# Transposes of the identity in TensorE's gaps up to the first step, with new due dates up to step 16

## Chip, cores and metric

One core of a Trainium2 chip. The metric is the device time of one execution in microseconds (us), the median over several runs. Engines: PE = TensorE, DVE = VectorE, ACT = ScalarE, POOL = GpSimd, SP = SyncE, which here only issues transfers.

## What is computed

A linear attention feeds a two-layer feed-forward block. With q, k, v of 8 batches, 8 heads, 576 rows, 64 columns, in float32 (eps is 1e-9):

```python
q_s = exp(q - max(q, over d));  q_s = q_s / (sum(q_s, over d) + eps)
k_s = exp(k - max(k, over s));  k_s = k_s / (sum(k_s, over s) + eps)
kv  = einsum('bhsd,bhse->bhde', k_s, v)
x   = einsum('bhsd,bhde->bhse', q_s, kv)      # heads side by side: 4608 x 512
h   = x @ w_in                                # w_in 512 x 2048
out = (s * relu(h)**2 + b) @ w_out            # w_out 2048 x 512
```

## The kernel before

**Tiling.** The rows of x are cut into nine blocks of 512: eight hold the first 512 rows of each batch, the ninth gathers the remaining 64 rows of all batches. The hidden size of 2048 is cut into 16 chunks of 128, so there are 9 x 16 = 144 steps. Every product of the feed-forward part is made in three pieces, high x high, high x low and low x high, since weights and x are each split into a rounded high part and a remainder. A step is 12 matmuls into one bank of PSUM, `h` (line 693), an elementwise chain over ACT and DVE that gives `gh` and `gl` (lines 718 to 735), and 12 matmuls into `acc` (line 760).

**The start.** Before step 0 the attention of batch 0 has to be done, in units `u` of two heads, two units to a pair. A unit of K (`k_stream`, line 324) is turned by five transposes on PE (`kT`, line 330), its maximum is taken on DVE (`km`, line 333), exp on ACT gives `ke` (line 338), five more transposes turn it back (`kn`, lines 343 and 344), and ACT copies it out (lines 346 and 347). A unit of q (`q_stream`, line 400) has its maximum, subtraction, exp, sum and scaling on DVE and ACT (lines 409 to 423), is turned on PE (`qT`, line 427), copied by ACT (`qf`, line 430) and multiplied by `kv` (`xp`, line 437); ACT and DVE then write x in its two parts (lines 443 and 446). `kv` itself is 20 small matmuls a pair (line 295). The transposes take the 128 x 128 identity `ident` as their second operand.

**The weights.** Each of the 16 chunks comes in two transfers of 512 KB (`load_w`, lines 180 and 182) and is converted by `conv_w` in seven operations on ACT and DVE (lines 196 to 219), chunk 0 in two halves. All of block 0's steps wait for these conversions, so that DVE's share of them falls into the first 16 steps, together with q and k of batch 1.

**Who sets the order.** Each piece of work is a generator of `Op`s (engine, estimated cost, due date, what it needs, which buffers it takes and frees). `Order.run` (line 142) plays them through on a model clock before anything is built: it takes the `Op` that can start earliest and, among those of its engine that can start within `NEAR` of it, the one with the smallest due date; it then emits its instructions. Every engine executes its list in that order and waits on semaphores. `DUE_K`, `DUE_Q`, `DUE_V` and `DUE_W` (lines 44 to 47) hold the due dates of the units, in steps. `COLD` is the model time up to which PE's costs count twice. `transfers` (line 803) gives the order of the first loads on SP's queue; q of pair 0 comes on ACT's. The tag `h` stands for one bank of PSUM, taken first by step 0.

Of the kernel before, what the change touches and what calls it, by code (L numbers as in the profile page):

```python
# [8 lines left out]
F32 = mybir.dt.float32  # L9
# [17 lines left out]
def attention_moe(ctx: ExitStack, tc: tile.TileContext, q, k, v, w_in, w_out, s, b, out):  # L27
    nc = tc.nc
# [3 lines left out]
    P = 128  # L32
# [8 lines left out]
    AHEAD = 1.5  # L41
    PACE = 6

    DUE_K = (-30, 0.5, -20, -25, 3.5, 11.5, 12, 19.5)
    DUE_Q = (-18, -32.5, -13.5, -6, 12.5, 9, -30.5, 64.5)
    DUE_V = (-81.5, -28.5, -14, 31)
    DUE_W = -15
    assert DM == H * D and DM == NP * P and 2 * D == P and 2 * LEFT == P and B * LEFT == TB

    const = ctx.enter_context(tc.tile_pool(name="const", bufs=1))  # L50
# [6 lines left out]
    ps = ctx.enter_context(tc.tile_pool(name="ps", bufs=1, space=bass.MemoryType.PSUM))  # L57


    ident = const.tile([P, P], F32, name="ident")  # L60
# [20 lines left out]
    def by_head(t):  # L81
        return t[:, 0:KQ].rearrange("p (h n d) -> p h n d", h=4, d=D)
# [21 lines left out]
    class Op:  # L104
# [4 lines left out]
        def __init__(self, eng, cost, due, needs=(), take=(), free=(), gives=(), kb=0, late=0.0):  # L109
            self.eng, self.cost, self.due, self.kb, self.late = eng, cost, due, kb, late  # L110
            self.needs, self.take, self.free, self.gives = needs, take, free, gives

    class Order:

        NEAR, HOP, TRIP, RATE = 0.1, 0.15, 2.8, 0.33
        COLD = 18

        def __init__(self, bufs):  # L120
            self.bufs = bufs
            self.at, self.done, self.pipe = {}, {}, 0.0
            self.taken = {tag: 0 for tag in bufs}
            self.freed = {tag: [] for tag in bufs}

# [16 lines left out]
        def run(self, streams):  # L142
            heads = [[next(g), 0.0, g] for g in streams]
            while heads:
                can = [(self.start(o, ready), i) for i, (o, ready, g) in enumerate(heads)]
                can = [(t, i) for t, i in can if t is not None]
                first, i = min(can)
                eng = heads[i][0].eng
                t, i = min(
                    ((t, i) for t, i in can if heads[i][0].eng == eng and t <= first + self.NEAR),  # L150
                    key=lambda c: (heads[c[1]][0].due, c),
                )
                o, ready, g = heads[i]

                heads[i][1] = end = self.at[eng] = t + o.cost * (2 if eng == "PE" and t < self.COLD else 1)
                if o.kb:
                    self.pipe = max(self.pipe, end) + o.kb / 1024 / self.RATE
                    end = self.pipe + self.TRIP
                for tag in o.take:
                    self.taken[tag] += 1  # L160
                for tag in o.free:
                    self.freed[tag].append(end + self.HOP)
                for n in o.gives:
                    self.done[n] = end, "DMA" if o.kb else eng
                heads[i][0] = after = next(g, None)
                if after is None:
                    del heads[i]
                elif not o.kb and (eng != "PE" or after.eng != eng):
                    heads[i][1] = end + self.HOP
# [15 lines left out]
    def conv_w(f, some):  # L185

        due = f - AHEAD if f else DUE_W
        n = some.stop - some.start
# [130 lines left out]
    def wide(u):  # L319

        return ("acc", 2) if u < NP else ("big", 1)

    def k_stream(u):
        pr, i = divmod(u, 2)
        due, (tag, bufs) = DUE_K[u], wide(u)
        yield Op("PE", 0.6, due, needs=[f"k{u} there"], take=["big", "ke"])
# [22 lines left out]
    def k_pair(pr):  # L349
        us = (2 * pr, 2 * pr + 1)  # L350
        due = DUE_K[us[0]]

        def sm(n):
            return ps.tile([P, 512], F32, name=f"{n}_{pr}", tag="sm", bufs=1)

        yield Op("DVE", 1.13, due, needs=[f"k{u} there" for u in us])
        kt = by_head(tiles[pr][0])
        kts = [kt[:, 2 * i:2 * i + 2] for i in range(2)]
        m2, m1, km = k_tiles(pr)
        k_max_2(kt, m2)  # L360
        yield Op("DVE", 0.9, due)
        k_max_1(kt, m2, m1)
        yield Op("PE", 0.25, due, take=["sm"])
        kT = sm("kT")
        k_turn(m1, kT)
        yield Op("DVE", 0.35, due, free=["sm"])
        k_top(kT, km)
        yield Op("PE", 0.25, due, take=["sm"])
        mb = spread(km, sm("mb"))
        for i, u in enumerate(us):  # L370
            yield Op("DVE", 0.73, due, free=["sm"] if i else (), gives=[f"k{u} less"])
            k_less(kts[i], mb, i)
        for i, u in enumerate(us):
            yield Op("ACT", 0.63, due, gives=[f"k{u}"])
            k_exp(kts[i])

    def kv_second(pr):
        due = DUE_V[pr]
        yield Op("PE", 1.4, due, needs=[f"k{u}" for u in (2 * pr, 2 * pr + 1)] + [f"v{pr} there"], take=["sm"], gives=[f"kv{pr}"])
# [7 lines left out]
    def kv_stream(pr):  # L387
        us = (2 * pr, 2 * pr + 1)
        due = DUE_V[pr]
        yield Op("DVE", 0.5, due, needs=[f"z{u}" for u in us])  # L390
# [9 lines left out]
    def q_stream(u):  # L400
        pr, i = divmod(u, 2)
        bb, hp = divmod(u, NP)
        due, (tag, bufs) = DUE_Q[u], wide(u)

# [398 lines left out]
    def transfers():  # L803

        yield from some_k(0, 0)
        yield from some_k(0, 1)
        yield from fetch(0)
        yield from some_k(1, 0)
        yield from some_k(1, 1)
        yield from whole(1, 1, "q")  # L810
        yield from whole(0, 2, "v")
        yield from whole(1, 2, "v")
        for f in range(1, NFE):
            yield from fetch(f)

    def some_k(pr, i, due=0, needs=()):
        yield Op("SP", 1.9, due, needs=needs, gives=[f"k{2 * pr + i} there"], kb=480)
        load_k(pr, i)

    def whole(pr, which, n, due=0, needs=()):  # L820
        gives = [f"k{2 * pr} there", f"k{2 * pr + 1} there"] if which == 0 else [f"{n}{pr} there"]
        yield Op("SP", 1.3, due, needs=needs, gives=gives, kb=576)
        load_heads(pr, which, nc.sync)
# [13 lines left out]
    def fetch(f):  # L837
        yield Op("SP", 0.65, f, needs=[f"w{f - NFE} 2 read"] if f >= NFE else (), take=["w"], gives=[f"w{f} 0 there"], kb=512)
        load_w(f, 0)
        yield Op("SP", 0.65, f, gives=[f"w{f} 1 there"], kb=512)  # L840
        load_w(f, 1)

    def reload(pr):

        p = 0 if pr == NP // 2 else pr - 1
        due = DUE_K[2 * pr] - 2

# [6 lines left out]
    def reload_late(pr):  # L854
# [17 lines left out]
        return k_(), q_(), v_()  # L872

    tiles.update({pr: raws[pr % 2 if pr < 2 else 0] for pr in range(NU // 2)})
    order = Order({
        "acc": 2, "big": 1, "sm": 1, "h": 1, "r": 1, "g": 2, "ke": 1, "qf": 1, "qe": 2, "m2": 1, "m1": 1, "top": 1,
        "maxima": 2, "turned": 2, "xleft": 2, "tmp": NTMP, "w": NFC + 1
    })
    E = mybir.EngineType
    late = range(NP, NU // 2)  # L880
    with tc.manual_schedule(engines={E.PE, E.DVE, E.Activation, E.Pool, E.SP}):
# [42 lines left out]
```

## Time and profile before

| | |
|---|---|
| median of 3 runs | 880.31 us (879.52 to 880.44) |
| the profiled execution, its own time | 879.32 us |
| its span, first to last instruction | 877.5 us |
| PE busy | 855.6 us, 97% of the span |
| DVE busy | 497.5 us, 57% |
| ACT busy | 356.9 us, 41% |
| DMA | 79.43 MB, mean 91 GB/s |

The profiled execution takes 1.8 us more than its span, for what lies around the first and the last instruction. Shares are over the whole span; the start and the long run of steps have different limits, so stretches are read apart. The ends of matmuls are modelled, and a time in a row of several instructions (x5) runs from the start of the first to the end of the last. "Idle before" names the event that came last ahead of an instruction.

### The profile page before, as it was taken

The numbers are of one execution on the slowest core, as the hardware profiler recorded it, in microseconds if no ns is written. First come the engines' busy times: TensorE is split into PE (matmuls) and PEld (weight loads), VectorE is DVE, ScalarE is ACT, GpSimd is POOL, SyncE is SP. The second block draws the span as 40 slices with busy tenths as digits, with TensorE's granted clock in tenths as the row PEclk, the third lists the DMA queues.
The fourth block names the chain that finished last, engine by engine and source line by source line (L and its number), as shares of the span: only waits on it lengthen the run. The fifth ranks groups of instructions, "written<-read, shape, count | busy, mean of one in ns | idle before, by whom it ended". The sixth has DMA issues, their size and how long they took to land.

```text
span 877.5 us, 11329 instructions
## 1 busy us (share of the span) xinstructions
PE 855.6 (97%) x4360; PEld 705.5 (80%) x4360; DVE 497.5 (57%) x799; ACT 356.9 (41%) x568; POOL 90.9 (10%) x110
## 2 busy tenths in 40 slices
PE   4899999999999999999999999999999999999997
PEld 4677887888888888888888888888888888888886
DVE  7999997566665656564566536663652232232222
ACT  5988854434433333333333333433342322222222
POOL 1000002121121202020112002120200010000000
PEclk9999999999999999999999999999999999999999
DMA  9968034533433414341433243321411000000001
GB/s 246 309 245 269 2 83 119 126 87 86 132 85 110 108 59 109 108 110 36 132 85 85 84 129 88 85 85 70 116 32 52 12 37 1 1 24 25 1 1 48
DMA packets 109957, 79.43 MB, mean 91 GB/s; under 512 B 60624, under 2 KB 103632, under 8 KB 109776
## 3 DMA queue, kind: packets, MB, share of 16 engines
q1 hardware_dynamic: 108496, 77.60, 32.2%
q10 hardware_dynamic: 1408, 1.12, 0.4%
q8 instruction: 34, 0.56, 0.3%
q14 instruction: 19, 0.16, 0.1%
HBM read 60.29 MB, written 18.40 MB: 90 GB/s over the span
## 4 chain that ended last, share of the span: by engine, by line
PE 86%; DVE 6%; DMA 2%; ACT 2%; issue 2%; SPq 1%; ACTq 0%; DVEq 0%
PE acc L760 41%; PE h L693 40%; PE kv L295 2%; PE xp L650 2%; DMA q<-in_q_dram 1%; DMA v<-in_v_dram 1%; DVE low L212 1%; DVE w L219 1%; SPq L284 1%; DVE st L209 1%; DVE low L202 1%; PE xq L650 1%; DVE st L207 0%; ACT st L199 0%; ACT low L196 0%
## 5 line engine op out<-in xcount | busy, mean ns | idle before, releaser
L693 PE MATMUL h<-x,w 128*128 128x512 f32 x1728 | 419.7, 391 | 3.0 <-DVE x L446 1.0
L693 PEld LDWEIGHTS h<-x,w 128*128 128x128 f32 x1728 | 322.6, 188 | 72.4 <-DVE w L219 1.9
L760 PE MATMUL acc<-w,gh 128*128 128x512 f32 x1152 | 357.3, 391 | 0.0
L760 PEld LDWEIGHTS acc<-w,gh 128*128 128x128 f32 x1152 | 214.8, 188 | 45.3 <-ACT o L786 0.4
L731 DVE SCALAR_TENSOR_TENSOR r<-r,sb 128x512 f32<-128x512 f32 x136 | 106.1, 780 | 253.7 <-ACT r L718 253.0
L760 PE MATMUL acc<-w,gl 128*128 128x512 f32 x576 | 224.7, 390 | 0.2 <-DVE gl L735 0.2
L718 ACT ACTIVATE r<-h 128x512 f32<-128x512 f32 x144 | 86.1, 598 | 319.2 <-PE h L693 313.2
L735 DVE SCALAR_TENSOR_TENSOR gl<-r,sb,gh 128x512 fp32r<-128x512 f32 x136 | 106.9, 786 | 60.4 <-ACT gh L733 59.5
L733 ACT ACTIVATE gh<-r,sb 128x512 fp32r<-128x512 f32 x136 | 98.4, 724 | 88.6 <-DVE r L731 88.0
L760 PEld LDWEIGHTS acc<-w,gl 128*128 128x128 f32 x576 | 108.1, 188 | 23.9 <-DVE gl L735 0.9
L572 POOL TENSOR_TENSOR q<-q,qm 128x640 f32<-128x640 f32 x24 | 35.8, 1502 | 133.3 <-DVE qm L570 133.2
L589 POOL TENSOR_TENSOR qe<-qe,qr 128x640 f32<-128x640 f32 x24 | 31.5, 1316 | 32.0 <-DVE qr L585 12.4
L659 DVE TENSOR_TENSOR x<-xp,x 128x512 fp32r<-128x512 f32 (+1 forms) x24 | 13.3, 553 | 20.8 <-ACT x L657 20.3
L576 ACT ACTIVATE qe<-q 128x640 f32<-128x640 f32 x24 | 18.7, 785 | 15.5 <-POOL q L572 15.5
L295 PEld LDWEIGHTS kv<-v,k 128*64 128x64 f32 x600 | 19.8, 143 | 6.0 <-issue 2.8
L635 POOL TENSOR_TENSOR kvhl<-kvf,kvhl 128x256 fp32r<-128x256 f32 x12 | 8.9, 741 | 133.9 <-issue 127.3
L295 PE MATMUL kv<-v,k 128*64 128x65 f32 (+1 forms) x600 | 21.9, 230 | 0.7 <-DMA v<-in_v_dram 0.7
L593 DVE STREAM_TRANSPOSE q<-qe 128x640 f32<-128x640 f32 x24 | 19.6, 818 | 4.5 <-POOL qe L589 4.5
L579 DVE TENSOR_REDUCE qs<-qe 128x20 f32<-128x640 f32 x24 | 19.0, 794 | 5.1 <-ACT qe L576 5.1
L559 ACT ACTIVATE k<-k 128x640 f32<-128x640 f32 x24 | 17.2, 736 | 11.3 <-DVE k L521 11.3
L561 POOL MEMSET k<- 64x128 f32 x24 | 4.8, 200 | 154.5 <-ACT k L559 152.2
L607 DVE TENSOR_TENSOR qT<-qT,qh 128x640 fp32r<-128x640 f32 x24 | 19.7, 821 | 1.7 <-ACT qh L604 1.7
(111 smaller groups left out, 527.9 us busy)
## 6 DMA issues: line engine op xcount, KB each, us to landing
st<-in_moe_w_in_dram SPq DMA_DIRECT2D x16, 512.0 KB, 8.9
st<-in_moe_w_out_dram SPq DMA_DIRECT2D x16, 512.0 KB, 8.9
out_dram<-o SPq DMA_DIRECT2D x16, 512.0 KB, 2.7
turned<-q SPq DMA_DIRECT2D x24, 320.0 KB, 2.4
qT<-turned SPq DMA_DIRECT2D x48, 160.0 KB, 4.3
q<-in_q_dram SPq DMA_DIRECT2D x14, 512.0 KB, 5.3
k<-in_k_dram SPq DMA_DIRECT2D x14, 512.0 KB, 4.3
v<-in_v_dram SPq DMA_DIRECT2D x56, 128.0 KB, 4.9
```

Source lines behind the costliest of these rows:

```text
L295: nc.tensor.matmul(kv[h * D:(h + 1) * D, i], kt[:, i, h, n], vt[:, 2 * i + h, n], start=(n == 0), stop=(n == NT - 1))
L572: nc.gpsimd.tensor_tensor(out=qt, in0=qt, in1=bc(qm, [P, 2, NT, D]), op=ALU.subtract)
L589: nc.gpsimd.tensor_tensor(out=qe_, in0=qe_, in1=qr, op=ALU.mult)
L593: nc.vector.transpose(out=tb, in_=qe.rearrange("p h t n r -> p (h t n r)"))
L607: nc.vector.tensor_tensor(out=ql, in0=qT, in1=qh.bitcast(F32), op=ALU.subtract)
L650: nc.tensor.matmul(t[:, 0:n * D], lhs, rhs[:, a, 0:n], start=(j == 0), stop=(j == len(terms) - 1))
L693: nc.tensor.matmul(hp_, w[:, j, c, :], x[:, c, :], start=(c == 0 and i == 0), stop=(c == NP - 1 and i == 2))
L718: nc.scalar.activation(r, hp_, AF.Relu)
L731: nc.vector.scalar_tensor_tensor(out=r, in0=r, scalar=s_col, in1=r, op0=ALU.mult, op1=ALU.mult)
L733: nc.scalar.activation(gh, r, AF.Identity, bias=b_col)
L735: nc.vector.scalar_tensor_tensor(out=gl, in0=r, scalar=b_col, in1=gh.bitcast(F32), op0=ALU.add, op1=ALU.subtract)
L760: nc.tensor.matmul(acc[blk, j // 2][:, j % 2], g[:, js], w_, start=(f == 0 and i == 0), stop=(f == NFC - 1 and i == 2))
```

## The change

In `Order.run`, whenever the next `Op` in the model is one of PE's, the model's gap on PE ahead of it is handed to a new function `idle`, which emits plain transposes of the identity into a tile `unused` with tag `h`, as many as fill 60% of the gap at 0.109 us each. With the first `Op` that takes `h`, step 0's, the tile is let go and no more are emitted. PE's model clock begins at 3.0, `COLD` goes from 18 to 8, `NEAR` from 0.1 to 0.05. The due dates of the K, q, V units and of chunk 0 are new (of the four tables the diff shows two), two estimated costs of `k_pair` are lowered, and in `transfers` chunk 0 of the weights moves behind K of unit 3, which itself moves behind the V of both pairs.

```diff
-    DUE_K = (-30, 0.5, -20, -25, 3.5, 11.5, 12, 19.5)
...
-    DUE_W = -15
+    DUE_K = (-44.5, 19.5, -45.5, 24.5, 10.5, 60, -2, -2)
...
+    DUE_W = -82
...
-        NEAR, HOP, TRIP, RATE = 0.1, 0.15, 2.8, 0.33
-        COLD = 18
-
-        def __init__(self, bufs):
-            self.bufs = bufs
-            self.at, self.done, self.pipe = {}, {}, 0.0
+        NEAR, HOP, TRIP, RATE = 0.05, 0.15, 2.8, 0.33
+        COLD = 8
+
+        def __init__(self, bufs, idle):
+            self.bufs, self.idle = bufs, idle
+            self.at, self.done, self.pipe = {"PE": 3.0}, {}, 0.0
...
                 o, ready, g = heads[i]
+                if eng == "PE":
+
+                    self.idle(t - self.at[eng], "h" in o.take)
...
-        yield Op("DVE", 1.13, due, needs=[f"k{u} there" for u in us])
+        yield Op("DVE", 0.69, due, needs=[f"k{u} there" for u in us])
...
-        yield Op("DVE", 0.9, due)
+        yield Op("DVE", 0.85, due)
...
         yield from some_k(0, 0)
         yield from some_k(0, 1)
-        yield from fetch(0)
         yield from some_k(1, 0)
-        yield from some_k(1, 1)
         yield from whole(1, 1, "q")
         yield from whole(0, 2, "v")
         yield from whole(1, 2, "v")
+        yield from some_k(1, 1)
+        yield from fetch(0)
...
+    unused = [ps.tile([P, 512], F32, name="unused", tag="h")]
+
+    def idle(us, last):
+        if last:
+            unused.clear()
+        for _ in range(int(0.6 * us / 0.109) if unused else 0):
+            nc.tensor.transpose(unused[0][:, 0:P], ident, ident)
+
     order = Order({
...
-    })
+    }, idle)
```

The lines of the code below the tables move by three, those below the planner's call by more: 330 becomes 333, 409 becomes 412, and so on.

**PE, the middle of the stage ahead of step 0.** Names ahead of the arrow are what is written; numbers in them count buffers. Before:

```order
L330 MATMUL kT_174<-ident,k_91 128x128 x5
L427 MATMUL qT_186<-ident,qe_137 128x128 x5
L343 MATMUL kn_206<-ident,ke_197 128x128 x4
L344 MATMUL kn_206<-ident,ke_197 64x128
L330 MATMUL kT_222<-ident,raw_90 128x128 x5
L295 MATMUL kv_242<-v_93,k_91 64x64 x20
L343 MATMUL kn_271<-ident,ke_265 128x128 x4
L344 MATMUL kn_271<-ident,ke_265 64x128
L330 MATMUL kT_280<-ident,raw_90 128x128 x5
```

Now:

```order
L884 MATMUL unused_101<-ident 128x128 x5
L346 MATMUL kn_238<-ident,ke_226 128x128 x4
L347 MATMUL kn_238<-ident,ke_226 64x128
L333 MATMUL kT_248<-ident,k_91 128x128 x5
L884 MATMUL unused_101<-ident 128x128 x16
L346 MATMUL kn_294<-ident,ke_270 128x128 x4
L347 MATMUL kn_294<-ident,ke_270 64x128
L333 MATMUL kT_309<-ident,raw_90 128x128 x5
L298 MATMUL kv_318<-v_93,k_91 64x64 x20
```

The fourth `kT` (`kT_280` before, `kT_309` now) stands ahead of the first `kv` instead of behind it, and 16 transposes of the identity stand between the third `kT` and the `kn` ahead of the fourth.

**SP's queue, the loads behind the first unit of K** (`k_91` is K of pair 0, `raw_90` holds K, q and V of pair 1, `st` a chunk of weights). Before:

```order
L269 DMA k_91<-in_k_dram 64x2x64
L180 DMA st_116<-in_moe_w_in_dram 128x4x256
L182 DMA st_116<-in_moe_w_out_dram 128x1024
L268 DMA raw_90<-in_k_dram 128x4x64 x2
L269 DMA raw_90<-in_k_dram 64x2x64
L268 DMA raw_90<-in_k_dram 128x4x64 x2
L269 DMA raw_90<-in_k_dram 64x2x64
L274 DMA raw_90<-in_q_dram 128x4x256
L275 DMA raw_90<-in_q_dram 64x4x64
L274 DMA v_93<-in_v_dram 128x4x256
L275 DMA v_93<-in_v_dram 64x4x64
L274 DMA raw_90<-in_v_dram 128x4x256
```

Now:

```order
L271 DMA raw_90<-in_k_dram 128x4x64 x2
L272 DMA raw_90<-in_k_dram 64x2x64
L277 DMA raw_90<-in_q_dram 128x4x256
L278 DMA raw_90<-in_q_dram 64x4x64
L277 DMA v_93<-in_v_dram 128x4x256
L278 DMA v_93<-in_v_dram 64x4x64
L277 DMA raw_90<-in_v_dram 128x4x256
L278 DMA raw_90<-in_v_dram 64x4x64
L271 DMA raw_90<-in_k_dram 128x4x64 x2
L272 DMA raw_90<-in_k_dram 64x2x64
L183 DMA st_209<-in_moe_w_in_dram 128x4x256
L185 DMA st_209<-in_moe_w_out_dram 128x1024
```

Chunk 0 of the weights comes last of this group instead of third, and the second K unit of pair 1 follows q and both V.

**DVE, rows 196 to 201 of its list**, where the first operations of batch 2 (`m_4`) and those of step 15 (`gl`) meet. Before:

```order
L455 TENSOR_TENSOR m_4_1310<-k_91 128x512
L491 TENSOR_TENSOR m_4_1311<-m_4_1310 128x256
L492 TENSOR_TENSOR m_4_1311<-m_4_1311,k_91 64x256
L728 TENSOR_TENSOR gl_1297<-r_1295,gh_1296 128x512
L496 STREAM_TRANSPOSE m_4_1310<-m_4_1311 128x256
L446 TENSOR_TENSOR x_956<-xp_1317,x_956 128x512
```

Now:

```order
L458 TENSOR_TENSOR m_4_1381<-k_91 128x512
L494 TENSOR_TENSOR m_4_1382<-m_4_1381 128x256
L495 TENSOR_TENSOR m_4_1382<-m_4_1382,k_91 64x256
L731 TENSOR_TENSOR gl_1365<-r_1363,gh_1364 128x512
L499 STREAM_TRANSPOSE m_4_1381<-m_4_1382 128x256
L449 TENSOR_TENSOR x_1133<-xp_1385,x_1133 128x512
```

From row 196 on the two lists read alike here; the 195 rows ahead are the same operations in another order.

## Rows read from the trace of the kernel before

**Rows 1.** The page: busy time by engine; busy tenths of DVE in 40 slices.
```profile
PE 855.6 (97%) x4360; PEld 705.5 (80%) x4360; DVE 497.5 (57%) x799; ACT 356.9 (41%) x568; POOL 90.9 (10%) x110
...
DVE  7999997566665656564566536663652232232222
```

**Rows 2.** Stretches: length, busy PE, PEld, DVE, ACT, POOL, granted clock, DMA share, GB/s.
```profile
22.31:26.00 3.69, 2.63 (x15) 2.10 (x13) 2.29 (x4) 2.85 (x8) 0.00 (x0) 1.00 1.09 325
26.00:40.00 14.00, 10.68 (x82) 7.51 (x83) 13.86 (x26) 13.76 (x22) 0.00 (x0) 1.00 1.04 312
40.00:133.78 93.78, 92.36 (x480) 74.15 (x479) 92.69 (x138) 74.88 (x99) 1.50 (x4) 1.00 0.50 157
133.78:866.00 732.22, 732.22 (x3686) 607.65 (x3686) 370.29 (x597) 251.44 (x416) 86.42 (x88) 1.00 0.27 72
...
6.33:133.78 127.45, 116.64 (x649) 93.33 (x650) 124.61 (x198) 101.14 (x146) 1.95 (x6) 1.00 0.64 195
```

**Rows 3.** Waits of DVE from 6 to 134 us: us in total, times, longest.
```profile
DVE qm L409 <- DMA q<-in_q_dram: 6.3, 1, 6.3
DVE km L333 <- PE kT L330: 1.0, 1, 1.0
DVE w L219 <- ACT w L217: 0.6, 2, 0.4
DVE x L446 <- ACT xleft L237: 0.4, 1, 0.4
```

**Rows 4.** Timeline of DVE: start, us, instruction, idle before.
```profile
23.27 0.76 DVE L333 TENSOR_REDUCE km<-kT 128x1 f32<-128x576 f32 x1 [0.96 <-PE kT L330]
...
25.89 0.17 DVE L301 TENSOR_SCALAR z<-z 128x2 f32<-128x2 f32 x1
...
26.70 0.76 DVE L411 TENSOR_TENSOR raw<-raw,qm 128x640 f32<-128x640 f32 x1
...
136.06 0.69 DVE L728 TENSOR_TENSOR gl<-r,gh 128x512 fp32r<-128x512 f32 x1 [2.28 <-ACT gh L726]
```

**Rows 5.** Timeline of PE, 0 to 45 us.
```profile
10.93 1.12 PE L343 MATMUL kn<-ident,ke 128*128 128x128 f32 x4 [2.68 <-ACT ke L338]
...
16.54 1.27 PE L330 MATMUL kT<-ident,raw 128*128 128x128 f32 x5
18.50 2.40 PE L295 MATMUL kv<-v,k 128*64 128x64 f32 x40 [0.69 <-DMA v<-in_v_dram]
20.83 1.12 PE L343 MATMUL kn<-ident,ke 128*128 128x128 f32 x4
...
21.95 1.27 PE L330 MATMUL kT<-ident,raw 128*128 128x128 f32 x5
23.02 1.36 PE L437 MATMUL xp<-qf,kvf 128*128 128x256 f32 x4
24.22 0.71 PE L427 MATMUL qT<-ident,qe 128*128 128x128 f32 x5
```

**Rows 6.** Issues on SP's queue (start, us), and time from issue to landing of the same transfers.
```profile
15.22 0.60 SPq L275 DMA_DIRECT2D raw<-in_v_dram  x1
...
23.80 0.99 SPq L182 DMA_DIRECT2D st<-in_moe_w_out_dram  x1
...
raw<-in_v_dram SPq DMA_DIRECT2D x1, 64.0 KB, 5.5
...
st<-in_moe_w_out_dram SPq DMA_DIRECT2D x1, 512.0 KB, 11.4
```

**Rows 7.** Timeline of ACT, 0 to 45 us.
```profile
10.05 0.74 ACT L338 ACTIVATE ke<-kT,km 128x576 f32<-128x576 f32 x1
...
10.78 0.67 ACT L196 ACTIVATE low<-st 128x512 int32<-128x512 uint32 x1
...
12.30 0.59 ACT L346 COPY k<-kn 128x512 f32<-128x512 f32 x1
...
17.42 0.62 ACT L217 CAST w<-low 128x512 fp32r<-128x512 f32 x1
```

More of the change, by code (lines that the diff above doesn't have):

```diff
@@ L42, in attention_moe @@
     PACE = 6
-    DUE_K = (-30, 0.5, -20, -25, 3.5, 11.5, 12, 19.5)
-    DUE_Q = (-18, -32.5, -13.5, -6, 12.5, 9, -30.5, 64.5)
-    DUE_V = (-81.5, -28.5, -14, 31)
-    DUE_W = -15
+    DUE_K = (-44.5, 19.5, -45.5, 24.5, 10.5, 60, -2, -2)
+    DUE_Q = (-32, -38, -23, -28, 12.5, 10.5, -70, 68)
+    DUE_V = (-82, -23, -10.5, 20.5)
+    DUE_W = -82
     assert DM == H * D and DM == NP * P and 2 * D == P and 2 * LEFT == P and B * LEFT == TB
```

## The prediction

> **What bounds the kernel now.** I began with the page: TensorE (PE) is busy for 97% of the span, so a gain can only come from where PE idles, and the slices put that at the very start, where VectorE (DVE) shows nines or nearly so for five slices [rows 1]. The table of stretches then splits the span at 133.78 us. Behind it PE is busy for 732.22 of 732.22 us: nothing can be won there, and the end moves only with the moment at which this stretch begins. Ahead of it, from DVE's first instruction at 6.33 us, DVE runs 198 instructions and is busy for 124.61 of 127.45 us, PE for 116.64 [rows 2]. The order lists of DVE give the meaning of the cut: in both kernels the same 198 rows, in another order, stand ahead of row 199, where DVE waits 2.28 us for step 15's `gh` [rows 4], PE being the one behind from there. So **DVE sets the start of the steady stage**. Its work up to there is unchanged, its first instruction waits for the same first load of q (6.3 us [rows 3]), and what the change can save is DVE's idle time in between: 127.45 - 124.61 = 2.84 us, 0.3% of the time. That is the ceiling. PE allows hardly more: from 40 us to the cut it idles 93.78 - 92.36 = 1.42 us [rows 2], and some microseconds ahead of 40.
>
> Who causes these 2.84 us is in the list of DVE's waits: 1.0 us for the fourth transposed K tile (PE), 0.4 for a copy of x (ACT), 0.6 for two copies of a weight (ACT), 2.0 us in all [rows 3]. The other 0.8 are gaps of hundredths between small instructions that depend on each other; the 198 rows keep them.
>
> The chain of waits on the page also names a load of q and one of v; this is the view's habit of taking the latest event, and DVE's list has no wait for either.
>
> **TensorE's clock.** Five transposes take 1.27 us at 16.54 and at 21.95 us but 0.71 at 24.22, with the same shapes; without the length of the last one that is 0.21 for each in one case and 0.11 in the other, the ratio of 1.2 to 2.4 GHz [rows 5]. The granted clock reads 1.00 in all stretches [rows 2], so this step has to be read from the durations. The rise falls into the four matmuls at 23.02. Before it PE had been busy without a break since 18.50, 2.3 us with kv matmuls and 2.2 with transposes; transposes alone, those from 10.93 on and those up to 17.8, had not brought it [rows 5].
>
> **The change, part by part.**
>
> *The filling.* 67 transposes of the identity in eight runs (24, 10, 2, 5, 16, 1, 1, 8), on PE alone, into a bank that nobody reads before step 0 takes it. At the fast clock 67 x 0.11 = 7 us, at the slow one 67 x 0.21 = 14 us. The first 24 (5.1 us slow) run from about 2 us, when the identity is there, to about 7.1, about when the first real transposes start; with the kT transposes and the next ten PE is then busy without a break from 2 to about 10 us. The rise in the trace came after 5 us of unbroken work, so I take the clock to rise between 5 and 10 us instead of at 23.5. What it pays: PE's own work in this stage lies beside DVE's. The wait of 1.0 for kT goes, as the order puts the fourth kT ahead of kv (2.40 us) and the clock halves it; the 0.4 for x goes too, since it hung on the same slow PE.
>
> The filling has no cost where it ends before its gap does. The tightest is the run of 16 behind the third kT. While it runs, the maximum (0.76), exp and its read-out (0.74 and about 0.2) must pass on DVE and ACT, 1.7 us with their steps [rows 4, 7]; 16 x 0.11 = 1.75 us. It is a draw. DVE has some 2.9 us of work from this maximum to the next (0.7 for itself, 0.8 for five small ones as from 25.89 to 26.70, twice 0.7 for 640 columns [rows 4]), and the next kT needs 1.7 + 1.25 (ten transposes of 0.11 and a tail) = 2.95 until it is there: no wait, or 0.1.
>
> The Trainium skill, "TensorE: Matmul & The Clock Gate", section "Part 4: PE-mode transpose", says that transposes do not count as busy for the clock as matmuls do. By it the filling would not raise the clock, and the sum would be that of the first rival below. The trace here leaves it open, as told: half of the unbroken stretch ahead of the rise were transposes, yet the two stretches of transposes alone saw no rise.
>
> *The loads.* The first weights (1 MB, two transfers) move on SP's queue from behind the second K tile to behind the fourth, so the third K tile, q and v come earlier by about 3 us, and the fourth K tile, now behind q and v, later by as much; its transposes stand behind the run of 16 and have time. The bytes up to the end of this group are the same as before, so weights 0 now land when v of the second pair does: 15.22 + 5.5 = 20.7 us for the second half, and 1.7 us earlier for the first (512 KB at the 312 GB/s of [rows 2]), at 19.0 [rows 6]. They used to be worked on from 10.78 [rows 7]. ACT then has 0.67 for low, 0.59 and a smaller one for kn copies, 0.67 again: 21.1 us. DVE gets there after 28 rows, eighteen of about 0.7, one of half that and nine of 0.1 to 0.2, some 14.5 us in all, at 20.8 to 21. New wait: 0 to 0.7, I take 0.3.
>
> Behind this, DVE's subtraction for the first weight waits for ACT's cast (0.62), which is queued behind an exp and the last kn copies: I take 0.45, between 0 and 0.8. One row sum later waits for an exp behind the same queue: 0.3, between 0 and 0.5 [rows 7].
>
> The reload of q for the second batch moves behind weights 4. The bytes up to its end are about those up to the end of the transfer issued at 23.80, which lands 11.4 us later: 35.2 [rows 6]. DVE's first row on it is row 55, and by the same count the 54 rows ahead end at about 35. Wait: 0 to 0.9, I take 0.2.
>
> *The planner.* New due dates, a cost of 0.69 for 1.13, tolerance and cold phase change no instruction; they only choose the order. The two copies of weights that DVE waited for (0.6 [rows 3]) meet another order; in the new one the casts stand several rows ahead of their readers, so I count these waits as gone.
>
> **Sum.** Away: 1.0 + 0.4 + 0.6 = 2.0. New: 0.1 + 0.3 + 0.45 + 0.3 + 0.2 = 1.35. Net -0.65 us. With all new waits at nothing -2.0, with all at their upper end (3.0) +1.0. The profiled execution took 879.32 us, so 878.7; the median of the runs shown stands 0.99 above it, so **879.7** for the median. From no change a measurement of this kernel can tell 0.2%, that is 1.76 us: under 878.55 or over 882.07.
>
> **Rivals.**
>
> *The filling does not raise the clock (slower), 0.12.* Then it is 14 us of slow work in front of real work on an in-order queue. At the run of 16: 3.4 us instead of 1.75, then kn and kT in 2.3: 5.7 us after the third kT against DVE's 2.9 and 0.4 for its start behind the last transpose's tail, a wait of 2.4. Two shorter ones come at the run of 10 and at those of 2 and 5, 0.3 to 0.5 each: 3.2 new against 2.0 gone, while the waits on ACT are then hidden: +1.2. If the clock rises only some 5 us after the start of the kv matmuls, near 28 us, then these (2.40 us, half of it too much) and ten transposes more (0.1 each too much) stay slow: up to +3.4. So 881.5 to 883.7. It decides if the third kT still takes 1.27 us. For it: the transposes without a rise. Against it: those from 20.83 to 23.0 lay directly ahead of the rise and kept PE as busy as the filling will [rows 5].
>
> *The late weights eat the gain, 0.14.* ACT becomes the one waited for at 21 to 28 us, and q's reload comes late: new waits of 1.9 to 3.0, so 880.2 to 881.3. For it: ACT is busy for nearly all of 26 to 40 us already (13.76 of 14.00 [rows 2]). Against it: between 19 and 26 us ACT has room, 2.85 of 3.69 us busy from 22.31 to 26 [rows 2].
>
> *All waits go, 0.12.* -2.0, at the ceiling -2.84: 877.5 to 878.3. For it: each of the new waits is under half a microsecond and rests on a landing that I know to 0.5. Against it: three of them hang on one queue, ACT's, behind the same late load.
>
> That the change doesn't do what it says is excluded: the fillings stand in PE's order.
>
> **Numbers.** The forecast (a gain of 0.1 to 1.6, 878.7 to 880.2) has 0.62. The range from 878.3 to 881.6 leaves out most of the last rival and most of the first, 0.2 together. Faster by more than 0.2%: the last rival and the forecast's edge, 0.15. Slower: two thirds of the first rival and a little, 0.09. The rest, 0.76, is within 0.2%.
>
> **What would show it.** Right: the second kT of the new kernel takes 0.71 us; DVE's busy time up to its row 199 is 124.6 again and its idle there about 2.2; waits for PE are gone from DVE's list and ACT leads it, with the first weights at 21 to 25 us; PE stays full behind. Wrong: fillings of 0.21 us after 10 us, a DVE wait of 2 us for kT near 21, or the steady stage beginning at 133.8 or later.

## The result, and the profile after

The change takes 882.49 us (median of 11 runs, 879.97 to 883.38) against 880.03 for the kernel before on the same chip (11 runs, 877.83 to 880.63): a ratio of 1.003, with a 95% interval of 1.0020 to 1.0039. It is slower by 0.3%, outside the range that was given. The profiled execution took 882.47 us with a span of 880.6, where before it was 879.32 and 877.5. One run below, of e3b_fill_only_on, took 960.97 us at a mean clock of 0.849 and is left out of its numbers.

The page of the kernel after: busy time by engine, and the 40 slices of TensorE's granted clock.

```profile
PE 863.4 (98%) x4427; PEld 712.9 (81%) x4427; DVE 501.5 (57%) x799; ACT 355.7 (40%) x568; POOL 87.7 (10%) x110
...
PEclk9899999999999999999999999999999999999999
```

PE has its 67 matmuls more, DVE the same 799 instructions. New is the 8 in the second slice of the clock (22 to 44 us). Cut as in [rows 2] at DVE's row 199, and finer at that slice (columns as there: stretch, length, PE, PEld, DVE, ACT, POOL, granted clock, DMA share, GB/s):

```profile
6.07:136.56 130.49, 120.23 (x699) 96.47 (x697) 125.54 (x198) 100.60 (x146) 1.56 (x6) 0.97 0.62 190
...
136.56:866.00 729.44, 729.44 (x3673) 605.43 (x3674) 372.57 (x597) 250.33 (x416) 83.62 (x88) 1.00 0.27 72
...
37.00:38.00 1.00, 0.34 (x1) 0.02 (x1) 1.00 (x2) 1.00 (x2) 0.00 (x0) 1.00 0.82 143
...
39.00:40.00 1.00, 1.00 (x4) 0.81 (x3) 1.00 (x2) 0.98 (x1) 0.00 (x0) 0.50 0.92 98
...
45.00:46.00 1.00, 1.00 (x5) 0.77 (x5) 1.00 (x2) 0.00 (x0) 0.00 (x0) 0.83 1.05 384
```

Behind the cut PE is full as before (729.44 of 729.44). So the loss lies ahead of it, as in the prediction's frame: DVE's 198 rows now take 130.49 us, of which 125.54 busy and 4.95 idle, against 127.45, 124.61 and 2.84. And from 38 to 46 us the granted clock is down, at 0.50 from 39 to 45: 1.2 GHz in place of 2.4. The timeline of PE of the kernel after (start, us, instruction, idle before) shows what went ahead:

```profile
2.02 5.38 PE L884 MATMUL unused<-ident 128*128 128x128 f32 x24 [2.02 <-POOL ident masks.py:199]
7.19 1.01 PE L333 MATMUL kT<-ident,k 128*128 128x128 f32 x5
...
11.27 0.71 PE L333 MATMUL kT<-ident,raw 128*128 128x128 f32 x5
...
34.38 1.24 PE L440 MATMUL xp<-qf,kvf 128*128 128x256 f32 x4
36.84 0.50 PE L696 MATMUL h<-x,w 128*128 128x512 f32 x1 [1.23 <-ACT x L446]
38.42 2.44 PE L696 MATMUL h<-x,w 128*128 128x512 f32 x5 [1.08 <-DVE x L449]
41.55 4.78 PE L696 MATMUL h<-x,w 128*128 128x512 f32 x12 [0.69 <-ACT r L721]
```

The filling did raise the clock early: the second kT, at 11.27, takes 0.71 us instead of 1.27. But between the end of `xp` at 35.6 and 38.4 us PE runs one matmul of half a microsecond, and then the clock falls: the twelve `h` of step 1, each of 512 columns, take 4.78 us. In the kernel before three of step 0's `h` run directly behind the last `xp`, those of step 1 take 3.02 us, and there is no fall in its stretch from 26 to 40 or behind it [rows 2]:

```profile
35.12 1.10 PE L693 MATMUL h<-x,w 128*128 128x512 f32 x3
...
39.35 3.02 PE L693 MATMUL h<-x,w 128*128 128x512 f32 x12 [0.69 <-ACT r L718]
```

The waits of DVE in the kernel after, behind its first load and up to 137 us (us in total, times, longest), and its row 199 in the timeline:

```profile
DVE gl L731 <- ACT gh L729: 1.3, 1, 1.3
DVE st L210 <- ACT st L202: 0.8, 1, 0.8
DVE r L734 <- ACT r L721: 0.7, 1, 0.7
DVE w L222 <- ACT w L220: 0.6, 2, 0.4
DVE low L205 <- ACT low L199: 0.4, 1, 0.4
DVE qs L420 <- ACT qe L417: 0.3, 1, 0.3
```

```profile
139.02 0.69 DVE L731 TENSOR_TENSOR gl<-r,gh 128x512 fp32r<-128x512 f32 x1 [2.46 <-ACT gh L729]
```

The waits for kT and `xleft` of [rows 3] are gone. In their place stand the first weights (`st`, `low`, `w`, and `qs` behind the same queue: 2.1 us) and, new, 0.7 us at 41.53 and 1.3 at 50.07, behind the slow `h` of steps 0 and 1. Row 199 starts at 139.02 instead of 136.06 [rows 4], 2.96 us later. Its ledger: idle +2.11, busy +0.93, the wait of row 199 itself +0.18, and -0.26 since the first row starts at 6.07 instead of 6.33. The span is 3.1 us longer.

### The profile page after: what moved, and what is told of

Same layout as the page of the kernel before. It is cut to its first block, busy times and chain, and to the rows that moved or that the text cites. A ratio compares the mean times of both kernels' runs of the same rounds, so it can differ in the third digit from the quotient of the medians.

```text
span 880.6 us, 11466 instructions
## 1 busy us (share of the span) xinstructions
PE 863.4 (98%) x4427; PEld 712.9 (81%) x4427; DVE 501.5 (57%) x799; ACT 355.7 (40%) x568; POOL 87.7 (10%) x110
## 3 DMA queue, kind: packets, MB, share of 16 engines
q10 hardware_dynamic: 1408, 1.12, 0.4%
## 4 chain that ended last, share of the span: by engine, by line
PE 89%; DVE 5%; DMA 2%; issue 1%; ACT 1%; SPq 1%; DVEq 0%; ACTq 0%
PE h L696 42%; PE acc L763 42%; PE kv L298 2%; DMA st<-in_moe_w_in_dram 2%; PE xp L653 2%; DVE w L222 1%; DVE st L212 1%; PE xq L653 1%; DVE st L210 1%; DMA k<-in_k_dram 1%; DVE low L215 1%; DVE low L205 1%; PE xp L440 0%; DVE gl L738 0%; ACT low L199 0%
## 5 line engine op out<-in xcount | busy, mean ns | idle before, releaser
L734 DVE SCALAR_TENSOR_TENSOR r<-r,sb 128x512 f32<-128x512 f32 x136 | 108.6, 798 | 252.7 <-ACT r L721 252.2
L575 POOL TENSOR_TENSOR q<-q,qm 128x640 f32<-128x640 f32 x24 | 33.5, 1408 | 129.6 <-DVE qm L573 129.6
```

What stands on the lines that cost most here:

```text
L575: nc.gpsimd.tensor_tensor(out=qt, in0=qt, in1=bc(qm, [P, 2, NT, D]), op=ALU.subtract)
L734: nc.vector.scalar_tensor_tensor(out=r, in0=r, scalar=s_col, in1=r, op0=ALU.mult, op1=ALU.mult)
```

## The experiments

Three theories went into the first four runs. A: the fall of the clock at 38 us costs the time. B: the late first weights cost it. C: a clock that rose early falls at about 38 us whatever PE does. The experiments were made in three groups (e1 to e3b, e5 to e8, e9 to e12), each on another chip; a ratio is always to the kernel before run beside them, which took 880.22, 880.05 and 879.98 us.

**e1_fill_on: the change, with its filling carried on behind the first `h` matmuls.** From there it goes into a spare bank until that bank is taken (1, 18 and 5 transposes).

```diff
-    def idle(us, last):
-        if last:
+    def idle(us, last, sm):
+        if last and len(unused) == 1:
+            unused[:] = [None, ps.tile([P, 512], F32, name="spare", tag="sm", bufs=1)]
+        elif sm and len(unused) == 2:
             unused.clear()
...
-            nc.tensor.transpose(unused[0][:, 0:P], ident, ident)
+            nc.tensor.transpose(unused[-1][:, 0:P], ident, ident)
```

> The change as it is, but the transposes of the identity go on behind the first use of the h bank, into the bank of tag sm, until that is taken again: 1, 18 and 5 more in the gaps of step 0 and ahead of step 1. Theory A (PE did next to nothing from 35.4 to 38.4 us, so the clock fell to 1.2 GHz from 38.2 to 45.4 us): the clock stays up, the matmuls of step 1 take 0.23 us instead of 0.43, twelve of them at 0.2 us are 2.4 us, so about 880.0, the same as before. Theory B (the late first weights and the new waits of DVE cost the time, the fall of the clock lies beside other work): no gain over the change, 882 to 883.

880.23 us (879.53 to 882.25), ratio to the kernel before 1.0005 (0.9996 to 1.0014): 2.3 us less than the change. Its timeline of PE, its stretches up to DVE's row 199 and from 39 to 45 us, and its waits of DVE behind the first load, up to 134 us:

```profile
35.28 2.13 PE L886 MATMUL spare<-ident 128*128 128x128 f32 x18
...
38.39 1.43 PE L696 MATMUL h<-x,w 128*128 128x512 f32 x5 [0.75 <-DVE x L449]
...
40.68 3.04 PE L696 MATMUL h<-x,w 128*128 128x512 f32 x12 [0.32 <-ACT r L721]
```

```profile
6.24:134.02 127.78, 119.42 (x725) 97.12 (x723) 125.43 (x198) 100.80 (x146) 1.57 (x6) 1.00 0.64 191
...
39.00:45.00 6.00, 5.68 (x28) 4.52 (x27) 6.00 (x9) 4.62 (x6) 0.00 (x0) 1.00 0.99 319
```

```profile
DVE st L210 <- ACT st L202: 0.7, 1, 0.7
DVE w L222 <- ACT w L220: 0.4, 1, 0.4
DVE qs L420 <- ACT qe L417: 0.3, 1, 0.3
```

Nothing of the useful work, its order or its loads differs from the change, but the gap is full, the clock stays at 1.00, the twelve `h` take 3.04 us and the waits of 1.3 and 0.7 are gone. C falls, since the clock rose as early as in the change. A holds: DVE idles 2.35 us (127.78 - 125.43) against 4.95. Only the profiled run has a trace. Nine of the other ten read a mean clock of 0.996 or 0.997, the fastest (879.53) and the slowest (882.25) among them, so falls remain in them at places that are not known. What is left of the change is no better than the kernel before: 0.49 us less idle, but 0.82 us more busy (124.61 there), so that row 199 starts at 136.48 for 136.06.

**e2_no_fill: the change without any filling**, its due dates, costs and loads kept.

```diff
-        for _ in range(int(0.6 * us / 0.109) if unused else 0):
+        for _ in range(0):
```

> The new due dates and loads alone, no transposes of the identity. Theory A: the clock is at 1.2 GHz until after the kv matmuls at 20 us or later; whether it falls again at 38 us is open. Without a fall 880 to 881.5, with one up to 884. Theory B: the filling matters little, 882 to 883, and the clock between 36 and 46 us is not what tells the two kernels apart.

883.13 us (882.15 to 883.5), ratio 1.0034 (1.0021 to 1.0046). The granted clock, by stretches:

```profile
20.00:24.00 4.00, 4.00 (x49) 3.55 (x47) 2.60 (x5) 3.87 (x8) 0.00 (x0) 0.50 1.05 372
...
38.00:40.00 2.00, 0.88 (x2) 0.57 (x3) 2.00 (x4) 2.00 (x2) 0.00 (x0) 0.74 0.73 153
40.00:42.00 2.00, 2.00 (x5) 1.02 (x4) 1.95 (x4) 1.36 (x2) 0.00 (x0) 0.50 1.06 329
```

Two falls, each where PE had little to do: one within the 3.01 us that PE idles ahead of its kn at 19.37, and again ahead of step 0's last `h`. So that gap comes from the new order, not from the filling; and the filling of the change removes the first fall but not the second.

**e3_fill_only: the kernel before with the filling alone** (24, 10, 3, 4, 5 and 2 transposes; old due dates, costs and loads).

```diff
+                if eng == "PE":
+
+                    self.idle(t - self.at[eng], "h" in o.take)
...
+        for _ in range(int(0.6 * us / 0.109) if unused else 0):
+            nc.tensor.transpose(unused[0][:, 0:P], ident, ident)
```

> The kernel before with the transposes of the identity alone, due dates and loads as before. Theory A: the clock rises before 10 us, DVE's waits for PE (1.0 and 0.4 us) go; PE has three to four times as many matmuls between 34 and 39 us as in the change, so the clock stays up: 878.0 to 879.0. Theory C (a clock that has risen early falls around 38 us whatever PE does): a fall of some 7 us as in the change, 881 to 882.

878.23 us (877.75 to 879.5), ratio 0.9984 (0.9975 to 0.9993): faster than both kernels. The timeline of PE, its granted clock by stretches, and all that DVE waits for up to 134 us:

```profile
2.03 4.45 PE L884 MATMUL unused<-ident 128*128 128x128 f32 x24 [2.03 <-POOL own L67]
6.72 0.74 PE L333 MATMUL kT<-ident,k 128*128 128x128 f32 x5 [0.24 <-DMA k<-in_k_dram]
...
12.59 1.33 PE L430 MATMUL qT<-ident,qe 128*128 128x128 f32 x5 [0.56 <-DVE qe L426]
...
38.39 3.02 PE L696 MATMUL h<-x,w 128*128 128x512 f32 x12 [0.69 <-ACT r L721]
```

```profile
16.00:19.00 3.00, 2.69 (x16) 2.25 (x16) 2.96 (x6) 1.65 (x4) 0.00 (x0) 0.50 1.13 297
...
36.00:40.00 4.00, 2.34 (x9) 1.65 (x10) 4.00 (x7) 3.75 (x6) 0.00 (x0) 1.00 1.05 200
```

```profile
DVE qm L412 <- DMA q<-in_q_dram: 6.6, 2, 6.1
DVE w L222 <- ACT w L220: 0.7, 2, 0.4
```

The waits of 1.0 for kT and 0.4 for `xleft` [rows 3] are gone, and step 1's twelve `h` start at 38.39 instead of 39.35. Here too the clock falls, ahead of the `qT` at 12.59, and rises again at 19 us; nobody waits for PE there, and the fall costs nothing that DVE's list shows.

**e3b_fill_only_on: the same, carried on as in e1_fill_on.**

```diff
-            nc.tensor.transpose(unused[0][:, 0:P], ident, ident)
+            nc.tensor.transpose(unused[-1][:, 0:P], ident, ident)
```

> As the one before, with the transposes going on into the bank of tag sm (5, 10, 4 and 7 more up to step 2). Theory A: as e3_fill_only, 878.0 to 879.0, since there is no fall to prevent. Theory C: 878.0 to 879.0 too if filling holds the clock, against 881 to 882 without.

878.5 us (877.77 to 879.64, ten runs), ratio 0.9982 (0.9973 to 0.9991): no different from e3_fill_only.

**e5_gap_only: the change with the carried-on filling alone**, nothing ahead of the first `h`.

```diff
-        for _ in range(int(0.6 * us / 0.109) if unused else 0):
+        for _ in range(int(0.6 * us / 0.109) if len(unused) == 2 else 0):
```

> The change with no filling before step 0 takes its bank, and with the spare filling behind the first h matmuls alone (1, 18 and 5 transposes). Theory A (the fall of the clock at 38 us costs the time): PE is kept busy from 35 us on, the clock does not fall at 38 to 45, and the time comes down from 883.1 of the change without any filling by 2 to 2.7 us, to 880.4 to 881.1; the early transposes, slow ones, and the fall at 19 to 28 us stay as they were there, and cost up to 1.7 us for kT. Theory C (an early risen clock falls at about 38 us whatever PE does) was against the first runs already; by it nothing is gained. Rival: the early filling is needed for what the late one gives, because DVE is later by its waits for kT and the 18 transposes then fall short of the gap: the clock falls again, 882.5 to 883.5.

880.54 us (880.22 to 881.75), ratio 1.0008 (1.0000 to 1.0017). By this the 24 transposes among and behind step 0's `h` are worth 2.6 us (883.13 to 880.54; 2.3 by the two ratios), and the early ones, beside them, not measurably anything (880.54 and 880.23). The waits of DVE, from the profiled run, which is the slowest of the eleven (881.75), show why the early ones bring so little:

```profile
DVE km L336 <- PE kT L333: 1.7, 2, 1.1
DVE kvf L313 <- PE kv L298: 0.4, 1, 0.4
```

Without early filling DVE waits 2.1 us for PE but, being later, not for the first weights; with it it waits 1.4 us for those.

**e6_weights_first and e7_old_loads: the weights earlier.** e1_fill_on with the first weights ahead of the fourth K tile:

```diff
-        yield from some_k(1, 1)
         yield from fetch(0)
+        yield from some_k(1, 1)
```

> The change with filling carried on (880.23), and the first weights ahead of the fourth K tile instead of behind it. Theory B (what is left of the waits behind the late first weights, 0.7 + 0.4 + 0.3 us, is a cost): the weights land 1.5 to 2 us earlier, DVE's waits for ACT go from 1.4 to 0.5 or less, and the time falls to 879.3 to 879.9, if the fourth kT, whose load is then late by as much, does not take their place. Rival: DVE waits as long for kT's load, 880.2 or more.

893.3 us (889.92 to 895.16), ratio 1.0146 (1.0127 to 1.0165). And e1_fill_on with all its transfers in the order of the kernel before:

```diff
         yield from some_k(0, 1)
+        yield from fetch(0)
         yield from some_k(1, 0)
+        yield from some_k(1, 1)
...
         yield from whole(1, 2, "v")
-        yield from some_k(1, 1)
-        yield from fetch(0)
```

> The change with filling carried on, its due dates and the planner's new costs, but the transfers in the order of the kernel before (first weights behind the second K tile, fourth K tile ahead of q and v). By theory B the waits behind the first weights go (1.1 to 1.4 us) and the time is 879 +/- 0.4 as long as the clock stays up; if the due dates themselves hold the loss, it stays at 880 to 881. If PE idles again for some 3 us ahead of step 0 or 1 and the clock falls, theory A says 881.5 to 883, with 512-column matmuls of 0.43 us in the place.

896.73 us (896.4 to 897.01), ratio 1.0192 (1.0179 to 1.0206). Neither came out as expected: 893.3 lies in the open range of the rival ("880.2 or more"), but DVE waits for no kT there. The due dates belong to one order of transfers; with another the loss arises far behind the place that was touched. Of e6_weights_first and of e7_old_loads, the stretch from 100 to 200 us:

```profile
100.00:200.00 100.00, 95.53 (x479) 76.13 (x478) 66.83 (x110) 42.89 (x71) 9.86 (x11) 0.95 0.31 76
```

```profile
100.00:200.00 100.00, 94.70 (x520) 75.60 (x519) 68.28 (x116) 43.93 (x73) 11.95 (x14) 1.00 0.33 86
```

PE idles 4.5 and 5.3 us there, where it idles 0.3 in e1_fill_on, and the clock is down for a part of it in e6_weights_first (0.95). In e7_old_loads it is down earlier (0.90 from 34 to 100 us). So the price of the late weights by itself stays open: it is known only by its waits.

**e8_fill_more: e3_fill_only with whole gaps instead of six tenths of them.**

```diff
-        for _ in range(int(0.6 * us / 0.109) if unused else 0):
+        for _ in range(min(int(1.0 * us / 0.109), 24) if unused else 0):
```

> The kernel before with filling alone, and filling of the gaps whole instead of six tenths of them (24, 18, 1, 5, 1, 7, 1, 1, 8, 4 transposes; the first run as before). In the kernel with filling alone the clock fell from 12.6 to about 18.5 us. Theory A in its narrow form (a fall costs only where DVE then waits for PE): the early fall goes, wholly or in part, and the time stays within 0.5 us of 878.2, since DVE waited for no PE work there. Rival (each slow stretch costs half its busy time): 1.5 to 2.5 us faster, 876 to 876.8. Rival (filling in the way of real work): 878.8 to 880, with DVE waits for kT of 0.3 us or more.

878.92 us (877.75 to 880.66), ratio 0.9989 (0.9981 to 0.9998). The early fall did go, as expected, with no gain. The median is that of the last rival, but its sign is missing: DVE waits for no kT. Unexpected was another fall, in the profiled run:

```profile
16.00:19.00 3.00, 1.53 (x14) 1.29 (x12) 2.90 (x7) 1.75 (x4) 0.00 (x0) 1.00 1.09 283
...
39.00:43.00 4.00, 3.83 (x10) 3.06 (x11) 4.00 (x6) 2.94 (x4) 0.00 (x0) 0.57 0.85 211
```

Its useful PE work there stands in the same order as in e3_fill_only, with the same gaps at step 0 (0.22 and 1.04 us for 0.23 and 1.02), and there the clock held. The 12 runs of e8_fill_more also tell the price: the five at a mean clock of 1.00 took 877.75 to 878.34 us, the other seven, at 0.995 to 0.998, 878.87 to 880.66. The change's own runs do the same: ten at 0.993 to 0.996 took 882.16 to 883.38, the one at 0.999 took 879.97.

**e9_fill_more_on and e10_fill_over.** e8_fill_more carried on behind the first `h`, with whole gaps (e9) and with half as many transposes again (e10, a factor of 1.5 in the same line).

> The kernel before with filling of the whole gaps that the planner sees (as the run before this one) and carried on behind the first h matmuls (1, 9, 16, 7 and 12 transposes into a spare bank). In the kernel without the carrying on, the profiled run fell to half the clock from 38 to 43 us and took 880.24; its five runs at a mean clock of 1.00 took 877.75 to 878.34, the others 878.87 to 880.66. Theory A (the fall in front of step 0 costs the time of those others): with the gap from 36 to 39 us filled the fall goes, all runs are within 877.7 to 878.5, the mean clock at 0.998 or more. Rival: the falls come from elsewhere and still spread the runs: median 878.9 again.

878.31 us (877.73 to 879.34), ratio 0.9987 (0.9978 to 0.9996). Mean clock 0.998 to 1.000 in all runs, and ten of eleven within 877.73 to 878.74: most of the spread of e8_fill_more is gone, the median not below that of e3_fill_only.

> The same, with half as many transposes again as the planner's gaps hold (1.5 gaps; runs of at most 24). Theory A: PE idles less still, no falls, and the steps start as early, 877.6 to 878.3. Rival: the filling now stands ahead of real work that is ready, each time by up to half a gap (0.3 to 1.2 us): DVE waits for kT or PE starts the steps later, 878.5 to 880.5.

880.46 us (880.06 to 881.48), ratio 1.0011 (1.0002 to 1.0020), with the mean clock at 0.998 or more in all runs: the rival's figure. Here the filling stands in front of real work, and the gain is gone. Its timeline of PE:

```profile
35.39 2.78 PE L886 MATMUL spare<-ident 128*128 128x128 f32 x24
...
39.81 3.01 PE L696 MATMUL h<-x,w 128*128 128x512 f32 x12
```

The twelve `h` start at 39.81, 1.4 us later than in e3_fill_only.

**e11_change_fill_more: e1_fill_on with whole gaps** (the line of e8_fill_more).

> The change with filling carried on and of whole gaps. With six tenths it took 880.23, its profiled run 879.73 at a clock of 1.00 throughout. If falls in its other runs cost time, 879.5 to 879.8 now. The late first weights stay (1.4 us of waits for ACT), so it cannot reach the kernel before with filling: 878.2 or less would be against that term.

881.04 us (880.29 to 882.01), ratio 1.0016 (1.0007 to 1.0025). The clock read 1.00 in every stretch of the profiled run, and yet this is slower than the kernel before. The expected 879.5 to 879.8 was wrong: with the clock up, the change's order gains nothing. DVE's waits for ACT behind the first weights are 2.3 us here (`low` 0.9, `st` 0.7, `w` 0.4, `qs` 0.3), against 1.4 in e1_fill_on, because the weights land later. ACT's first row on them:

```profile
21.36 0.66 ACT L199 ACTIVATE low<-st 128x512 int32<-128x512 uint32 x1 [2.51 <-DMA st<-in_moe_w_in_dram]
```

With the same list of transfers it starts at 20.08 in e1_fill_on, 20.29 in the change and 20.45 in e5_gap_only. So the term of the late weights also varies, by up to 1.3 us between profiled runs. Whether the longer filling itself costs something here was not separated from it.

**e12_old_gap_only: the kernel before with filling behind the first `h` alone** (5, 10, 4 and 7; the condition of e5_gap_only).

> The kernel before with filling behind the first h matmuls alone (5, 10, 4 and 7 transposes), none ahead. Theory A: its profiled run has no fall at 36 to 40 us, so filling there changes little: 880 +/- 0.3, DVE still waits 1.0 for kT and 0.4 for x. Rival: the usual run of the kernel before (880.05 at a mean clock of 0.997, against 877.91 in one at 1.00) has a fall there as the change has, and 878.3 to 879 comes out.

878.9 us (878.36 to 880.42), ratio 0.9992 (0.9983 to 1.0001). Not told apart from no change by its interval, though the median is the rival's (878.3 to 879). The waits are theory A's: 0.9 for kT and 0.2 for x are still there. The rival's ground can be read in the runs of the kernel before. Of the 83 made beside the experiments, 66 read a mean clock of 0.993 to 0.997 and took 879.45 to 881.62 us; the fourteen at 0.998 took 878.62 to 879.25, the three at 1.00 877.91, 879.52 and 879.56. Its profiled run, at 1.00, is thus not the usual one. A part of what filling gains over its median may be a fall in the usual run, whose place no trace shows.

## Why the prediction was wrong

**What bounds the kernel: held.** From the start of DVE's row 199 to the end of the span it takes 741.3 to 741.7 us in the profiled runs of twelve kernels, all but e6_weights_first and e7_old_loads: 877.5 - 136.06 before, 880.6 - 139.02 after, 877.9 - 136.48 in e1_fill_on, 876.4 - 135.08 in e3_fill_only, and so on. The whole difference is made ahead of it.

**The clock's rise: held.** It came within the first kT, which from 7.19 us takes 1.01 us, between the 1.27 and 0.71 of the two clocks [rows 5]: inside the 5 to 10 us of the forecast. The waits of 1.0 for kT and 0.4 for `xleft` went, as said. The Trainium skill, "TensorE: Matmul & The Clock Gate", section "Part 4: PE-mode transpose", would have it that transposes do not bring the full clock. Here 24 transposes of the identity and a few of k did, with no other matmul ahead; the trace does not agree.

**The step that failed first: "PE's own work in this stage lies beside DVE's".** The clock was taken as won once it had risen: the sum had a term for the rise and none for a fall, which made PE's work the one waited for again. The moved work left PE with one matmul between 35.6 and 38.4 us, the clock fell for 7 us, and DVE waited for step 0's `r` and for step 1's `gh`. These two waits are 2.0 of the 2.60 us of idle time between the change and e1_fill_on (4.95 and 2.35); the other 0.6 lies at the first weights and the casts. Between the medians it is 2.3 us. That the fall went with the gap and took these waits with it is shown by e1_fill_on, e2_no_fill and e5_gap_only.

Where the gap comes from can be read in the code, in one of the two tables that the diff above leaves out:

```diff
-    DUE_Q = (-18, -32.5, -13.5, -6, 12.5, 9, -30.5, 64.5)
...
+    DUE_Q = (-32, -38, -23, -28, 12.5, 10.5, -70, 68)
```

In both kernels six `h` of step 0 stand behind the last `xp`, those of q units 2 and 3, and a step always takes the units from 0 to 3. Before, unit 2 came ahead of unit 3 (due -13.5 and -6), so its three `h` had their x and ran at once. Now unit 3 comes first (-28 and -23). Its x is the first of these two rows of DVE in the kernel after, there at 35.27, but its `h` stand behind those of unit 2, which need the second:

```profile
34.59 0.68 DVE L449 TENSOR_TENSOR x<-xp,x 128x512 fp32r<-128x512 f32 x1
...
37.68 0.68 DVE L449 TENSOR_TENSOR x<-xp,x 128x512 fp32r<-128x512 f32 x1
```

So five of the six start only at 38.42. This is read from code and rows; no run swapped the two dates back. The forecast compared no order of x with the order in which step 0 takes it.

The Trainium skill, on the same page as above, "TensorE: Matmul & The Clock Gate", describes in its section "HAM oscillation — how this bites in real kernels", that PE's waits for data lower its clock again after it has risen; the falls of the change and of e2_no_fill agree with it.

**The second: "Its work up to there is unchanged".** The same 198 instructions keep DVE busy for 125.54 us in the change and 125.43 in e1_fill_on, but 124.61 before: 0.8 to 0.9 us more, which the forecast took as zero. The timelines of DVE show one way in which it comes about, first the kernel before, then the kernel after:

```profile
32.17 0.69 DVE L207 TENSOR_SCALAR st<-st 128x1024 f32<-128x1024 f32 x1
32.78 0.81 DVE L411 TENSOR_TENSOR q<-q,qm 128x640 f32<-128x640 f32 x1
33.50 0.69 DVE L209 TENSOR_SCALAR st<-st 128x1024 uint32<-128x1024 uint32 x1
```

```profile
31.99 0.69 DVE L210 TENSOR_SCALAR st<-st 128x1024 f32<-128x1024 f32 x1
32.72 0.70 DVE L212 TENSOR_SCALAR st<-st 128x1024 uint32<-128x1024 uint32 x1
33.45 1.23 DVE L215 CUSTOM_DVE_ANT_0 low<-st,low 128x2048 uint16<-128x2048 uint16 x1
```

Where the next instruction reads what the one ahead wrote, it starts 0.04 us after its end (32.72 - 32.68); where it doesn't, 0.08 us before it (32.78 - 32.86). Counted by instruction, 171 of the 197 starts behind the first come before the end of the one in front in the kernel before, 163 in the change and 166 in e1_fill_on. The overlaps add up to 14.8, 13.6 and 14.1 us: 0.7 us less in e1_fill_on is most of its 0.82. An instruction that has to wait for another engine loses its overlap too, and the change has three more such waits. Nothing was run that changed this alone, so it is argued and not shown. Across the kernels busy time mostly goes with the order: 124.5 to 124.8 us in six with the old one (before, e3_fill_only, e3b_fill_only_on, e8_fill_more, e9_fill_more_on, e12_old_gap_only), 125.2 to 125.5 us in five with the new (the change, e1_fill_on, e2_no_fill, e5_gap_only, e11_change_fill_more). But e10_fill_over has the old order and 125.19 us, so order is not all of it.

**The new waits.** The run of 16 and the reload of q: 0, for 0.1 and 0.2. The first weight's cast and the row sum: 0.36 and 0.3, for 0.45 and 0.3. The first weights: 1.2 us (`low` 0.4, `st` 0.8), for 0.3, the term that was mis-sized most. The timeline of ACT of the kernel after has the landing:

```profile
20.29 0.66 ACT L199 ACTIVATE low<-st 128x512 int32<-128x512 uint32 x1 [1.89 <-DMA st<-in_moe_w_in_dram]
```

20.29 instead of the 19.0 taken from the bytes ahead of it. Of the two old waits for casts that the sum counted as gone, the longer (0.43 at 49.68) is still 0.26 at 51.02 in the change; in e1_fill_on it is gone. In e1_fill_on, with no fall, DVE's idle time changed by -0.49 us, forecast -0.65; that part of the sum was sound, though the first weights alone cost 0.7 there for 0.3, and the busy time took the gain back.

**The rivals.** None was the one that came. The first had the right sign, and its range (881.5 to 883.7) holds the measured time, but that is luck: its mechanism was a clock that does not rise, and this one rose and did not stay. The second, late weights that eat the gain, has its time (880.2 to 881.3) met by e1_fill_on at 880.23, but not its waits: 1.4 us there for its 1.9 to 3.0, and the rest is the 0.8 us of longer busy time that it did not name. In e11_change_fill_more, where the weights land later still, the waits are 2.3. Of the signs that were named, the second kT of 0.71 us came; the busy time of 124.6 and the idle time of 2.2 did not, and the steady stage begins at 136.56.

**What beats both kernels** is the part of the change without the rest: the filling in the order of before, 878.23 us, and with whole gaps carried on 878.31, ten of whose eleven runs lie within 1.0 us.

## What to carry to other kernels

A clock that has been raised has to be kept: when an edit moves work, look in the new order for every place where the engine is left with little to do, behind the edit too, and put a price on a fall there, above all where somebody waits for what comes next. Compare the order in which pieces are made with the order in which they are taken: here a piece that was ready stood behind one that came last. Fill gaps with work that nobody waits for, but short of the gap: at half as many again the filling itself was the delay. And when one edit joins a filler, a new schedule and a new order of loads, run each alone; here the first alone was worth -0.16%, and the three together +0.3%.

## What the runs showed of the hardware

TensorE's clock went from 1.2 to 2.4 GHz during transposes alone: in e3_fill_only the 24 of the identity take 4.45 us, less than 24 at 0.21, and the kT behind them 0.74. In e2_no_fill it rose with no filling, behind `kT`, `kn` and `qT` alone: four transposes for `kn` take 1.12 us at 10.88 and 0.66 at 15.05. Nearly the same rows at the same times did not bring it in the kernel before. While it had not yet risen for the first time, the granted clock read 1.00 (in the kernel before at transposes of 0.21 us each [rows 2, 5]); after a later fall it read 0.50. And gaps at step 0 that agree to 0.02 us made the clock fall in the profiled run of e8_fill_more and not in that of e3_fill_only. The executions of e8_fill_more alone divide by their mean clock, 877.75 to 878.34 us at 1.00 against 878.87 to 880.66 below it.
